# One row of wo per partition loaded early by GpSimd, dealt unevenly over the DMA engines

## The chip, the cores and the metric

The kernel runs on one core of a Trainium2 chip. The metric is the device time of one execution in microseconds (us); the median of three runs stands for the kernel. The profile is one execution taken by the hardware profiler. Data comes from HBM through the 16 DMA engines of the core. A load that is issued by SyncE (SP), ScalarE (ACT) or GpSimd (POOL) is cut into pieces, and each engine works off its own pieces in order. PE is TensorE, DVE is VectorE.

## The reference

One decode step of a block: a layernorm of x (576 numbers), attention of 32 heads over a cache of 16384 keys and values, and a gated MLP beside it, all added up.

```
xn = _layernorm(x, axis=-1)
q = (xn @ wq).reshape(B, Sq, H, Dh)              # H, Dh = 32, 128
scores = einsum("bhqd,bhkd->bhqk", q, k_cache) * Dh**-0.5
o = einsum("bhqk,bhkd->bhqd", softmax(scores), v_cache)
return x + o.reshape(B, Sq, H * Dh) @ wo + (gelu(xn @ w_gate) * (xn @ w_up)) @ w_down
```

The caches are 256 MB each, all of it float32, and everything is read once: 587.6 MB.

## The kernel before, in words

SBUF holds three big slots, A, B and C, each 64 KB per partition. SP issues nearly all loads, in the order of the program, each one when the slot that it fills has been given back: first the weights wq, w_gate and w_up, then for each head 8 MB of keys into A or B and 8 MB of values into C. DVE multiplies and sums keys with the query, PE sums the values. While the last heads are worked off, SP fetches w_down into B and A, and wo behind it.

wo has 4096 rows of 576 numbers. Partition p holds the 32 rows 32p to 32p+31 (`wov`), so that wo is a table of 128 partitions by WO_T = 32 columns j, a column being one row of wo on each partition. The output is the sum over j of a product of one vector of 128 (`oT[:, j]`, the attention's output turned to lie over partitions) with column j. The columns arrive in pieces: 12 and 8 into slot A (`WO_A`), then, once PE has read the last values out of C, 5, 3, 2, 1 and 1 into C (`WO_C`, lines 267 to 271). Each piece has a semaphore of its own, and PE takes the pieces in that order in the loop at line 451.

A load whose destination is 128 partitions gives each DMA engine eight pieces, here eight rows; the load of one column is 128 rows of 2304 bytes, eight on each engine. A load counts as landed when all its engines are done.

The end of the program is a chain over engines. After column j = 25, the first of the piece with three columns, PE signals `s_hf`; DVE adds what two PSUM banks hold into `x2` (lines 369 and 370); PE adds `x2` to the last four accumulators (line 459) and goes through columns 28 to 31; DVE and ACT copy the result out, and ACT stores it. Columns from 26 on (`WO_Q` = 6) go to four accumulators of 144 numbers, the earlier ones to two of 288.

GpSimd only sets constants at the start and then has nothing to do.

Of the kernel before, what the change touches and what calls it, by code (L numbers as in the profile page):

```python
# [8 lines left out]
AF = mybir.ActivationFunctionType  # L9
# [3 lines left out]
P = 128  # L13
H, SK, DH = 32, 16384, 128
D, DF = 576, 4608
# [5 lines left out]
HALF = D // 2  # L21
# [7 lines left out]
WO_T = HD // P  # L29
# [3 lines left out]
LOW, HIGH = 16512, 225280  # L33
WD_B = 28
WO_A = (12, 8)
WO_C = (5, 3, 2, 1, 1)
WO_Q = 6


# [1 line left out]
def kernel(ctx: ExitStack, tc: tile.TileContext, x, k_cache, v_cache, wq, wo, wg, wu, wd, out):  # L41
    nc = tc.nc
    PE, DVE, ACT, SP, PL = nc.tensor, nc.vector, nc.scalar, nc.sync, nc.gpsimd
# [3 lines left out]
    def small(name, shape, where="low"):  # L47
        n = 4
        for s in shape[1:]:
            n *= s  # L50
        h = nc.alloc_sbuf_tensor_at(name, list(shape), F32, offset=at[where])
        at[where] += (n + 31) // 32 * 32
        assert at["low"] <= SLOTS[0] and at["high"] <= 229344
        return h.ap()

    def slot(name, i):
        return nc.alloc_sbuf_tensor_at(name, [P, SLOT], F32, offset=SLOTS[i]).ap()

    A, B, C = slot("slot_a", 0), slot("slot_b", 1), slot("slot_c", 2)
    bank = [nc.alloc_psum_tensor(f"bank{i}", [P, 512], F32).ap() for i in range(8)]  # L60
# [6 lines left out]
    same = small("same", [P, 32])  # L67
# [29 lines left out]
    on = small("on", [P, H])  # L97
    onx = small("onx", [P, P])
    oT = small("oT", [P, WO_T])
    o2 = small("o2", [P, HALF])  # L100
    oTz = small("oTz", [P, WO_Q, 32])
    one31 = small("one31", [1, 32])

    kv = k_cache.rearrange("b h (p n) d -> (b h) p (n d)", p=P)
# [5 lines left out]
    wov = wo.rearrange("(p t) f -> p (t f)", t=WO_T)  # L110
# [4 lines left out]
    def sem(name):  # L115
        return nc.alloc_semaphore(f"{name}_{next(count)}")

    def on_(inst, s, n=1):
        inst.wait_op(s, n, "sem-ge")
        return inst  # L120

    def take(eng, s, n=1):
        eng.wait_ge(s, n).then_inc(s, -n)  # L123
# [6 lines left out]
    def step(eng, inst, after=True):  # L130

        s = own.setdefault(id(eng), None)
        if s is None:
            s = own[id(eng)] = sem("own")
            ahead[id(eng)] = 0
        if after is True:
            after = (s, ahead[id(eng)]) if ahead[id(eng)] else None
        if after:
            on_(inst, *after)
        inst.then_inc(s, 1)  # L140
        ahead[id(eng)] += 1
        return s, ahead[id(eng)]
# [5 lines left out]
    def load(dst, src, s, eng=None):  # L148
        return (eng or SP).dma_start(dst, src).then_inc(s, 16)  # L149
# [21 lines left out]
    s_al, s_pl, s_po, s_mz, s_hf, s_end, s_out = (sem(n) for n in ("al", "pl", "po", "mz", "hf", "end", "out"))  # L171
# [4 lines left out]
    at_c = 0  # L176
    for n in WO_C:
        pieces.append((C, at_c, wov, lo, n))
        at_c, lo = at_c + n, lo + n
    s_tail = [sem("tail") for _ in pieces]  # L180
    acc = [B[:, k * D : (k + 1) * D] for k in range(2)]
    s_wd, s_k0, s_fin = sem("wd"), sem("k0"), sem("fin")

    pgb = bank[:3]
    qgb = bank[3:5]
# [60 lines left out]
    for half_k in range(2):  # L246
        k0 = slice(half_k * SLOT // 2, (half_k + 1) * SLOT // 2)
# [18 lines left out]
    take(SP, fA)  # L266
    for (t, to, src, lo, n), sm in zip(pieces[:-len(WO_C)], s_tail):
        load(t[:, to * D : (to + n) * D], src[:, lo * D : (lo + n) * D], sm)
    take(SP, fV)
    for (t, to, src, lo, n), sm in list(zip(pieces, s_tail))[-len(WO_C):]:  # L270
        load(t[:, to * D : (to + n) * D], src[:, lo * D : (lo + n) * D], sm)
# [5 lines left out]
                                         channel_multiplier=1))  # L277
    cleared = step(PL, PL.memset(whose[:, H:], 0.0), None)
    marked = step(PL, PL.memset(one31[:, 31:], 1.0))


    DVE.wait_ge(s_x, 16)
# [78 lines left out]
    for s in s_acc:  # L361
# [4 lines left out]
    step(DVE, DVE.tensor_mul(on, oall, rl))  # L366
    spread_o = step(DVE, DVE.tensor_mul(onx.rearrange("p (h r) -> p h r", r=4), on.unsqueeze(2).to_broadcast([P, H, 4]),
                                        quarter.unsqueeze(1).to_broadcast([P, H, 4])))
    step(DVE, DVE.tensor_add(x2[:64], x2[:64], half_b[1][64:, :HALF]), (s_hf, 1))  # L369
    x_added = step(DVE, DVE.tensor_add(x2[:64], x2[:64], half_b[0][:64, :HALF]))  # L370
    on_(DVE.tensor_copy(o2[:64, :QUART], acc4[:64]), s_end, 1).then_inc(s_fin, 1)  # L371
# [15 lines left out]
        done(ACT, ACT.activation(oall[:, bass.ds(h, 1)], pcb[:, :1], AF.Copy), own_a)  # L387
    give(ACT, s_al)
    step(ACT, ACT.activation(oT, bank[5][:, :WO_T], AF.Copy), (s_po, 1))
    turned = step(ACT, ACT.activation(oTz[:, :, 31], bank[5][:, WO_T - WO_Q : WO_T], AF.Copy), None)  # L390


    PE.wait_ge(*identity)
# [2 lines left out]
    for j in range(DJ):  # L396
        PE.matmul(bank[5][:, j : j + 1], xm[:, j, :], ones[:1, :1], start=True, stop=True)
    PE.matmul(bank[5][:, DJ : DJ + 1], xd.rearrange("o d s -> o (d s)"), ones[:1, :1], start=True,
              stop=True).then_inc(s_px, 1)
# [9 lines left out]
    with PE.Fori(0, H):  # L409
# [7 lines left out]
        for k in range(32):  # L417
            q = 32 * (k % 4)
            i = PE.matmul(PO[q : q + 4, :], pe[:, 4 * k : 4 * k + 4], C[:, k * 512 : (k + 1) * 512],  # L419
                          start=k < 4, stop=k >= 28)  # L420
# [11 lines left out]
    half = [[half_b[i][32 * (2 * i + j) : 32 * (2 * i + j) + 1, :HALF] for j in range(2)] for i in range(2)]  # L432
    quart = [acc4[32 * g : 32 * g + (1 if g % 2 else 32), :] for g in range(4)]

    def add_out(groups, lhs, w, last=False, after=None):
        n = D // len(groups)
        for k, gr in enumerate(groups):
            lo = k % 2 * HALF + k // 2 * n
            i = PE.matmul(gr, lhs[k % len(lhs)], w[:, lo : lo + n], start=id(gr) not in seen, stop=last)  # L439
            seen.add(id(gr))  # L440
            if after and k == 0:
                on_(i, *after)
        return i

    for k, j in enumerate(range(WD_B, WD_T)):
        add_out(half[j % 2], [hT[:, j : j + 1]], A[:, k * D : (k + 1) * D], after=None if k else (s_tail[0], 16))
    on_(PE.matmul(bank[5][:, :WO_T], onx, same, start=True, stop=True), *spread_o).then_inc(s_po, 1)
    for k in range(2):
        add_out(half[k], [ones[:, :1]], acc[k])
    PE.wait_ge(*turned)  # L450
    for (t, to, _, lo, n), sm in list(zip(pieces, s_tail))[1:]:
        for k, j in enumerate(range(lo, lo + n)):
            w = t[:, (to + k) * D : (to + k + 1) * D]
            if j == WO_T - 4:
                PE.wait_ge(*x_added)
                PE.wait_ge(*marked)
                for i, gr in enumerate(quart):
                    r, c = 32 * (i % 2), i // 2 * QUART
                    PE.matmul(gr, ones[r : r + 1, :1] if i % 2 else one31, x2[r : r + 1, c : c + QUART], start=False,  # L459
                              stop=False)  # L460
            whole = j < WO_T - WO_Q
            lhs = [oT[:, j : j + 1]] if whole else [oTz[:, j - WO_T + WO_Q, :], oT[:, j : j + 1]]
            i = add_out(half[j % 2] if whole else quart, lhs, w,
                        last=j >= WO_T - WO_Q - 2 if whole else j == WO_T - 1, after=None if k else (sm, 16))
            if j == WO_T - WO_Q - 1:
                i.then_inc(s_hf, 1)
    i.then_inc(s_end, 1)

# [33 lines left out]
```

## Time and profile before

| | |
|---|---|
| median of 3 runs | 1362.09 us (1362.01 to 1362.15) |
| the profiled execution | 1362.08 us, of which the span of the profile is 1360.6 us |
| moved | 587.60 MB on SP's queue, 432 GB/s over the span |
| DVE busy | 85% of the span |
| PE busy | 31% of the span |

The profile's queue numbers: q1 is SP's queue, q10 is ACT's, q8 and q14 are fetches of instructions. The busy share of the DMA engines is a mean over 16: a share of 0.25 is four of them at work.

### The profile page before, as it was taken

What the parts mean: (1) busy time and instruction counts of PE and PEld (TensorE: products, weight loads), DVE (VectorE), ACT (ScalarE), POOL (GpSimd) and SP (SyncE); (2) the same over time, 40 slices, a digit from 0 to 9 for tenths busy, and PEclk for the clock granted to TensorE, in tenths of its full rate; (3) what the DMA queues carried; (4) which work ended last, traced back from release to release, by engine and by line L of the source; (5) the groups of instructions that cost most, each with busy time, mean ns of one, the idle gap of its engine ahead of it and who ended that gap; (6) DMA issues with size and microseconds to landing.
All of it is one profiled execution on the core that took longest, in us unless ns stands there. A gap on an engine that the chain in (4) does not pass through costs nothing. (4 is left out here: it accounts for less than half of the span.)

```text
span 1360.6 us, 7958 instructions
## 1 busy us (share of the span) xinstructions
PE 428.4 (31%) x3000; PEld 139.6 (10%) x3000; DVE 1159.9 (85%) x200; ACT 71.9 (5%) x233; POOL 1.5 (0%) x13
## 2 busy tenths in 40 slices
PE   3530233333222333333213333332223333222237
PEld 1110111101000111100001111000001111000012
DVE  1169999999888988898888888998898889988992
ACT  0000000000000000000000000000000000000000
POOL 0000000000000000000000000000000000000000
PEclk9765666666556666665566666665566666655668
DMA  9999999999999999999999999999999999999998
GB/s 399 450 424 432 432 434 447 435 434 434 432 432 434 434 434 432 432 435 447 435 432 434 432 432 435 434 432 432 432 441 441 435 434 432 432 432 435 433 428 379
DMA packets 11824, 587.70 MB, mean 432 GB/s; under 512 B 1317, under 2 KB 1321, under 8 KB 1834
## 3 DMA queue, kind: packets, MB, share of 16 engines
q1 hardware_dynamic: 11808, 587.60, 99.8%
q8 instruction: 5, 0.08, 0.0%
q10 hardware_dynamic: 10, 0.01, 0.0%
q14 instruction: 1, 0.01, 0.0%
HBM read 587.60 MB, written 0.00 MB: 432 GB/s over the span
## 5 line engine op out<-in xcount | busy, mean ns | idle before, releaser
L419 PE MATMUL bank<-slot_c,pe 128*4 128x512 f32 x2048 | 292.4, 735 | 624.1 <-PEq L123 624.1
L220 DVE TENSOR_TENSOR slot_a<-slot_a,qs 128x16384 f32<-128x16384 f32 x16 | 275.6, 17226 | 33.5 <-DVEq L123 33.5
L220 DVE TENSOR_TENSOR slot_b<-slot_b,qs 128x16384 f32<-128x16384 f32 (+1 forms) x17 | 275.8, 16222 | 27.3 <-DVEq L123 27.2
L225 DVE TENSOR_REDUCE s<-slot_b 128x128 f32<-128x16384 f32 (+1 forms) x17 | 275.7, 16216 | 5.7 <-DVEq L123 5.7
L225 DVE TENSOR_REDUCE s<-slot_a 128x128 f32<-128x16384 f32 x16 | 275.5, 17220 | 5.6 <-DVEq L123 5.6
L419 PEld LDWEIGHTS bank<-slot_c,pe 128*4 128x4 f32 x2048 | 56.6, 98 | 832.8 <-issue 832.8
L385 ACT ACTIVATE o<-bank 128x512 f32<-128x512 f32 x32 | 19.1, 597 | 890.5 <-ACTq L123 890.5
L412 PE MATMUL bank<-ident,pm 128*1 128x128 f32 x32 | 11.9, 372 | 168.5 <-PEq L123 168.5
L424 PE MATMUL bank<-same,o 128*128 128x1 f32 x256 | 32.7, 249 | 28.9 <-PEq L123 28.9
L424 PEld LDWEIGHTS bank<-same,o 128*128 128x128 f32 x256 | 31.0, 191 | 57.7 <-issue 57.7
L210 PE MATMUL bank<-qh,ones 128*128 128x128 f32 x66 | 20.1, 396 | 51.4 <-PEq L123 51.4
L319 DVE TENSOR_TENSOR slot_c<-bank,same 128x396 f32<-128x396 f32 (+1 forms) x6 | 3.3, 558 | 37.7 <-PE bank L201 37.5
L229 DVE TENSOR_REDUCE nm<-bank 1x1 f32<-1x128 f32 x32 | 8.9, 279 | 21.5 <-DVEq L123 21.5
L414 PE MATMUL bank<-nm,ones 1*128 1x1 f32 x64 | 17.7, 343 | 18.5 <-PEq L123 18.5
L412 PEld LDWEIGHTS bank<-ident,pm 128*1 128x1 f32 x32 | 2.5, 79 | 175.2 <-issue 175.2
L359 DVE SCALAR_TENSOR_TENSOR slot_b<-slot_b,hT 128x576 f32<-128x576 f32 x26 | 19.0, 810 | 0.0
L414 PEld LDWEIGHTS bank<-nm,ones 1*128 1x128 f32 x64 | 15.9, 307 | 27.9 <-issue 27.9
L210 PEld LDWEIGHTS bank<-qh,ones 128*128 128x128 f32 x66 | 13.1, 248 | 54.6 <-issue 54.6
L305 DVE TENSOR_TENSOR slot_c<-bank,same 128x512 f32<-128x512 f32 x2 | 1.4, 692 | 20.1 <-PE bank L201 20.1
L227 DVE TENSOR_REDUCE pm<-s 128x1 f32<-128x128 f32 x32 | 9.2, 286 | 7.6 <-DVEq L123 7.6
L206 ACT ACTIVATE qh<-qd,whose 128x128 f32<-128x128 f32 x33 | 13.2, 401 | 41.6 <-DVE qd L309 28.2
L380 ACT ACTIVATE nb<-bank 128x1 f32<-128x1 f32 x32 | 5.5, 172 | 179.2 <-ACTq L123 179.2
(88 smaller groups left out, 134.8 us busy)
## 6 DMA issues: line engine op xcount, KB each, us to landing
slot_b<-in_A_k_cache_dram SPq DMA_DIRECT2D x2, 4096.0 KB, 22.4
slot_b<-in_B_w_down_dram SPq DMA_DIRECT2D x1, 8064.0 KB, 41.7
slot_b<-in_B_w_gate_dram SPq DMA_DIRECT2D x1, 6912.0 KB, 54.6
slot_a<-in_B_w_up_dram SPq DMA_DIRECT2D x1, 6912.0 KB, 39.5
slot_a<-in_A_wo_dram SPq DMA_DIRECT2D x1, 3456.0 KB, 35.6
slot_c<-in_B_w_gate_dram SPq DMA_DIRECT2D x1, 2304.0 KB, 28.0
slot_c<-in_B_w_up_dram SPq DMA_DIRECT2D x1, 2304.0 KB, 35.2
slot_a<-in_B_w_down_dram SPq DMA_DIRECT2D x1, 2304.0 KB, 27.8
```

Source lines behind the costliest of these rows:

```text
L206: ACT.activation(qh, qd4.rearrange("p j t -> p (j t)"), AF.Copy, scale=whose[:, bass.ds(h, 1)]).then_inc(s_r, 1)
L210: PE.matmul(pqb[:, :DH], ones, qh, start=True, stop=True).then_inc(qp, 1)
L220: done(DVE, DVE.tensor_mul(blk, blk, qs.unsqueeze(1).to_broadcast([P, n, DH])), own_d)
L225: done(DVE, DVE.tensor_reduce(S[:, i * n : (i + 1) * n], blk, axis=AX.X, op=ALU.add), own_d)
L227: DVE.reduce_max(pm, S, axis=AX.X).then_inc(s_pm, 1)
L229: DVE.tensor_reduce(nm, ptb[:1, :P], axis=AX.X, op=ALU.max, negate=True).then_inc(s_nm, 1)
L359: DVE.scalar_tensor_tensor(acc[k], B[:, bass.ds((2 * i + k + 2) * D, D)], hT[:, bass.ds(2 * i + k + 2, 1)], acc[k], op0=ALU.mult, op1=ALU. ...
L385: ACT.activation(o4, PO, AF.Copy).then_inc(s_o4, 1)
L412: PE.transpose(ptb[:1, :P], pm, ident).then_inc(s_pt, 1)
L414: PE.matmul(ptb[:, 256:257], ones[:1, :], nm, start=True, stop=True).then_inc(s_pb, 1)
L419: i = PE.matmul(PO[q : q + 4, :], pe[:, 4 * k : 4 * k + 4], C[:, k * 512 : (k + 1) * 512], start=k < 4, stop=k >= 28)
L424: i = PE.matmul(pcb[:, :1], o4[:, j * DH : (j + 1) * DH], same[:, j : j + 1], start=j == 0, stop=j == 3)
```

## The change

GpSimd, after its last constant, issues five loads. Three of them bring column 31 of wo, one row of wo per partition of the old layout, into a buffer of its own, `w31`. The rows are dealt out anew: 72 rows as 6 groups of 12, 48 rows as 4 groups of 12, 8 rows as 2 groups of 4. Ahead of the first and of the second of these stands a tiny load (8 rows of 8 bytes, then one number) into `aim`, whose content nothing uses. SP's first piece into slot C is shorter by one column (4 instead of 5), so that SP loads 31 columns. Since the rows of `w31` lie on other partitions than before, DVE copies `onx` into `onp` in the same new order (three copies, L383), PE turns `onp` into `oT[:, 31]` by a product of its own, and the product with `w31` comes ahead of the columns in C. The roles that columns 25 to 31 had are now those of 24 to 30. `o2` and `oTz` move to another place in SBUF to make room.

```diff
-WO_C = (5, 3, 2, 1, 1)
+WO_C = (4, 3, 2, 1, 1)
+WO_L = WO_T - 1
...
+    onp = small("onp", [P, P])
+    w31 = small("w31", [P, D])
+    aim = small("aim", [P, 4])
...
+    shares = ((0, 0, 10, 6, 12), (72, 6, 10, 4, 12), (120, 120, 2, 2, 4))
...
     marked = step(PL, PL.memset(one31[:, 31:], 1.0))
+    for (to, first, gap, k, n), skip in zip(shares, (8, 1, 0)):
+        if skip:
+            at_s, w_s = (0, 2) if skip > 1 else (2, 1)
+            load(aim[:skip, at_s : at_s + w_s], wd[:skip, :w_s], s_aim, PL)
+        src = wov[first // gap * gap : first // gap * gap + gap * n, WO_L * D :]
+        src = src.rearrange("(b a) f -> a b f", a=gap)[first % gap : first % gap + k]
+        load(w31[to : to + k * n, :], src, s_w31, PL)
...
+    for to, first, gap, k, n in shares:
+        base = first // gap * gap
+        dealt = step(DVE, DVE.tensor_copy(
+            onp[:, to : to + k * n].rearrange("p (a b) -> p a b", a=k),
+            onx[:, base : base + gap * n].rearrange("p (b a) -> p a b", a=gap)[:, first % gap : first % gap + k]),
+            spread_o if to == 0 else None)
...
-    on_(PE.matmul(bank[5][:, :WO_T], onx, same, start=True, stop=True), *spread_o).then_inc(s_po, 1)
+    on_(PE.matmul(bank[5][:, :WO_L], onx, same[:, :WO_L], start=True, stop=True), *spread_o)
+    on_(PE.matmul(bank[5][:, WO_L:WO_T], onp, same[:, WO_L:], start=True, stop=True), *dealt).then_inc(s_po, 1)
...
     for (t, to, _, lo, n), sm in list(zip(pieces, s_tail))[1:]:
+        if t is C and not to:
+            PE.wait_ge(s_aim, 32)
+            add_out(half[1], [oT[:, WO_L:]], w31, after=(s_w31, 48))
```

On GpSimd, at the start of the program (`aim` and `w31` as above, `w_99` being `w31`), these rows stand in the change; before, the first two were its last:

```order
L283 MEMSET whose 128x1
L284 MEMSET one_101 1x1
L153 DMA aim<-in_B_w_down_dram 8x2
L153 DMA w_99<-in_A_wo_dram 72x1x576
L153 DMA aim<-in_B_w_down_dram 1x1
L153 DMA w_99<-in_A_wo_dram 48x1x576
L153 DMA w_99<-in_A_wo_dram 8x1x576
```

Nothing stands behind the five loads on this engine. On PE, in the tail behind the last head, before:

```order
L447 MATMUL bank<-same,onx 128x32
L439 MATMUL bank<-slot_b,ones 1x288 x4
L439 MATMUL bank<-slot_a,oT 1x288 x40
L439 MATMUL bank<-slot_c,oT 1x288 x12
L439 MATMUL bank<-slot_c,oTz 32x144
```

and in the change:

```order
L465 MATMUL bank<-same,onx 128x31
L466 MATMUL bank<-same,onp 128x1
L457 MATMUL bank<-slot_b,ones 1x288 x4
L457 MATMUL bank<-slot_a,oT 1x288 x40
L457 MATMUL bank<-w_99,oT 1x288 x2
L457 MATMUL bank<-slot_c,oT 1x288 x10
L457 MATMUL bank<-slot_c,oTz 32x144
```

One product is new (L466), and two products moved from slot C's first piece to `w31`, ahead of it.

## Rows read from the trace of the kernel before

**Rows 1.** The page: span, DMA busy tenths in 40 slices, fetches of instructions.

```profile
span 1360.6 us, 7958 instructions
...
DMA  9999999999999999999999999999999999999998
...
q8 instruction: 5, 0.08, 0.0%
```

**Rows 2.** The chain that ended last: start us, us, what.

```profile
1342.62 13.12 DMA slot_c<-in_A_wo_dram
...
1355.78 0.68 PE bank L439 x5
...
1356.48 0.47 DVE x L369
...
1356.97 0.46 DVE x L370
...
1357.47 0.44 PE bank L459 x6
1357.91 1.16 PE bank L439 x28
...
1359.10 0.30 DVE o L371
```

**Rows 3.** Windows at the end: busy by engine, clock, DMA share, GB/s.

```profile
1356.40:1356.60 0.20, 0.20 (x10) 0.19 (x4) 0.12 (x1) 0.00 (x0) 0.00 (x0) 1.00 0.93 369
...
1357.00:1357.20 0.20, 0.00 (x0) 0.00 (x0) 0.20 (x1) 0.00 (x0) 0.00 (x0) 1.00 0.32 127
1357.20:1357.40 0.20, 0.00 (x0) 0.00 (x0) 0.20 (x1) 0.00 (x0) 0.00 (x0) 1.00 0.30 115
1357.40:1357.60 0.20, 0.13 (x4) 0.13 (x8) 0.02 (x1) 0.00 (x0) 0.00 (x0) 1.00 0.26 104
...
1358.00:1358.20 0.20, 0.20 (x12) 0.20 (x8) 0.00 (x0) 0.00 (x0) 0.00 (x0) 1.00 0.09 35
```

**Rows 4.** DMA packets of 1357.4 to 1357.9.

```profile
DMA packets 23, 0.05 MB, mean 101 GB/s; under 512 B 1, under 2 KB 1, under 8 KB 23
```

**Rows 5.** DMA queues of 44 to 50: packets, MB, share of 16 engines.

```profile
q8 instruction: 1, 0.02, 1.0%
```

**Rows 6.** DMA queues of 1350 to 1358.4, same columns.

```profile
q8 instruction: 1, 0.02, 0.7%
```

**Rows 7.** DMA queues of 1358.4 to 1361, same columns.

```profile
q8 instruction: 1, 0.02, 2.2%
q10 hardware_dynamic: 4, 0.00, 0.3%
```

**Rows 8.** Timeline of GpSimd, its last instruction: start us, us, what.

```profile
3.68 0.09 POOL L279 MEMSET one<- 1x1 f32 x1
```

**Rows 9.** Timeline of the tail on DVE and PE, idle time in brackets.

```profile
1341.81 1.02 PE L424 MATMUL bank<-same,o 128*128 128x1 f32 x8 [0.90 <-PEq L123]
...
1344.78 0.29 DVE L367 TENSOR_TENSOR onx<-on,quarter 128x128 f32<-128x128 f32 x1
...
1347.44 0.41 PE L447 MATMUL bank<-same,onx 128*128 128x32 f32 x2
...
1348.30 5.03 PE L439 MATMUL bank<-slot_a,oT 128*1 128x288 f32 x80
...
1353.65 1.62 PE L439 MATMUL bank<-slot_c,oT 128*1 128x288 f32 x20 [0.32 <-DMA slot_c<-in_A_wo_dram]
```

**Rows 10.** Timeline of PE at its last column.

```profile
1358.58 0.30 PE L439 MATMUL bank<-slot_c,oT 128*1 128x144 f32 x2
```

More of the change, by code (lines that the diff above doesn't have):

```diff
@@ L99 @@
     oT = small("oT", [P, WO_T])
-    o2 = small("o2", [P, HALF])
-    oTz = small("oTz", [P, WO_Q, 32])
+    o2 = small("o2", [P, HALF], "high")
+    oTz = small("oTz", [P, WO_Q, 32], "high")
+    onp = small("onp", [P, P])
+    w31 = small("w31", [P, D])
+    aim = small("aim", [P, 4])
     one31 = small("one31", [1, 32])
@@ L181 @@
     acc = [B[:, k * D : (k + 1) * D] for k in range(2)]
-    s_wd, s_k0, s_fin = sem("wd"), sem("k0"), sem("fin")
+    s_wd, s_k0, s_fin, s_w31, s_aim = sem("wd"), sem("k0"), sem("fin"), sem("w31"), sem("aim")
+    shares = ((0, 0, 10, 6, 12), (72, 6, 10, 4, 12), (120, 120, 2, 2, 4))
     pgb = bank[:3]
@@ L389 @@
     step(ACT, ACT.activation(oT, bank[5][:, :WO_T], AF.Copy), (s_po, 1))
-    turned = step(ACT, ACT.activation(oTz[:, :, 31], bank[5][:, WO_T - WO_Q : WO_T], AF.Copy), None)
+    turned = step(ACT, ACT.activation(oTz[:, :, 31], bank[5][:, WO_L - WO_Q : WO_L], AF.Copy), None)
     PE.wait_ge(*identity)
@@ L451 @@
     for (t, to, _, lo, n), sm in list(zip(pieces, s_tail))[1:]:
+        if t is C and not to:
+            PE.wait_ge(s_aim, 32)
+            add_out(half[1], [oT[:, WO_L:]], w31, after=(s_w31, 48))
         for k, j in enumerate(range(lo, lo + n)):
             w = t[:, (to + k) * D : (to + k + 1) * D]
-            if j == WO_T - 4:
+            if j == WO_L - 4:
                 PE.wait_ge(*x_added)
@@ L460 @@
                               stop=False)
-            whole = j < WO_T - WO_Q
-            lhs = [oT[:, j : j + 1]] if whole else [oTz[:, j - WO_T + WO_Q, :], oT[:, j : j + 1]]
+            whole = j < WO_L - WO_Q
+            lhs = [oT[:, j : j + 1]] if whole else [oTz[:, j - WO_L + WO_Q, :], oT[:, j : j + 1]]
             i = add_out(half[j % 2] if whole else quart, lhs, w,
-                        last=j >= WO_T - WO_Q - 2 if whole else j == WO_T - 1, after=None if k else (sm, 16))
-            if j == WO_T - WO_Q - 1:
+                        last=j >= WO_L - WO_Q - 2 if whole else j == WO_L - 1, after=None if k else (sm, 16))
+            if j == WO_L - WO_Q - 1:
                 i.then_inc(s_hf, 1)
```

## The prediction

> **What bounds the kernel now.** I read the page first. In all but the last of the 40 slices the DMA engines are at nine tenths or more [rows 1]: the kernel moves its bytes without a pause, and the reader is to see that no compute engine can be the bound before the tail. So only the tail, and how evenly the 16 engines reach it, can change the time. The chain that ended last comes next. It leaves the DMA at 1342.62 + 13.12 = 1355.74, when the piece with wo's columns 25 to 27 has landed, and from there runs through PE (0.68), two additions on DVE (0.47 and 0.46), PE with x (0.44) and PE with the last four columns (1.16) to the copies at 1359.10 [rows 2]. Nothing in it waits for another load, but the last load is close behind: PE starts on its last column at 1358.58 [rows 10], and DMA is at work until some time between 1358.0 and 1358.2 [rows 3].
>
> The windows at the end say who is late there. The DMA share is 0.93 until 1356.6, then 0.32, 0.30 and 0.26, and the last packets go before 1358.2 [rows 3]. A share of 0.26 is four engines of 16. So some eleven engines have finished their part of the last load before 1357.0, a fifth late one (0.30 × 16 = 4.8 engines) at about 1357.35, and four finish only at 1358.0 to 1358.2, about a microsecond after most. Each load counts as landed with its slowest engine, so those four set every landing of the tail, also that of 1355.74.
>
> Why four? The page counts five fetches of instructions [rows 1], and one of these runs after 1358.4 [rows 7], so four came before the end of the loads. A fetch costs its engine about a microsecond: 1.0% of 16 engines in 6 us is 0.96 us [rows 5], and 0.7% in 8.4 us is 0.94 us [rows 6]. Four fetches of 0.95 us and four engines a microsecond late fit each other. No view names the engine of a packet, so that fetches and late engines are the same is inferred.
>
> **The change part by part.** *SP's tail is one column shorter.* The price of a row is read where only the late engines work: from 1357.4 to 1357.9 there are 23 packets, one of them tiny [rows 4], so four engines do 22 rows in 0.5 us, 4 × 0.5 / 22 = 0.091 us a row. Every engine has eight rows less in the tail: −0.73 us in every landing from slot C's first piece on.
>
> *GpSimd's three loads give rows back, at the start.* An engine that carries 12 rows is 12 × 0.091 = 1.09 us behind for the rest of the program, since no slack follows [rows 1]; one with 4 rows 0.36 us, one with none 0. Against SP's eight, ten engines (6 + 4) are 0.36 us worse, two are 0.36 us better, and four are 0.73 us better. GpSimd is idle from 3.77 us on [rows 8], and the rows are needed only after 1353, so the issue itself waits for nobody and nothing queues behind it.
>
> *Five more completions, two tiny loads.* The trace has no load from GpSimd. The nearest row is the store: four packets on q10 in 0.3% of 16 engines in 2.6 us, 0.125 us [rows 7]. Two are rows of half the length (0.045 us each by the price above), which leaves 0.017 us for each of the other two. Five completions on each engine would be 0.09 us; the bounds are 0 and, with the whole packet's mean of 0.031 us, 0.16. The tiny rows are of the same size and go into that bound.
>
> *DVE's three copies* begin after `onx`, which ends at 1344.78 + 0.29 = 1345.07, and PE asks for it at 1347.44 [rows 9]. Three copies of at most 128x128, 0.29 us each by that same row, end by 1345.94. Free, with 1.5 us of cover.
>
> *PE* gets one more product (two instructions; eight such took 1.02 us, so 0.26 us) and takes `w31` (four instructions at 5.03 / 80 = 0.063, 0.25 us) ahead of slot C [rows 9]. Before, PE had stood idle for 0.32 us until 1353.65 for C's first piece. Now it is through slot A's rows at 1353.33 + 0.26 = 1353.59, through `w31` at 1353.84, and through the four columns of C's first piece (16 × 0.063) at 1354.85, if that piece has landed, which it has (1353.65 − 0.64 = 1353.01). The next piece lands at 1355.74 − 0.64 = 1355.10. So the additions on PE are hidden, but with only 0.25 us left. Were that cover gone, PE would be the bound and the gain would shrink by what PE is over.
>
> *Sum.* If the four late engines are those that get no rows: −0.73 + 0.09 = −0.64 us on the landing at 1355.74, and all of the chain behind it moves by as much. The last load moves with it, and PE's last column too, so their order holds. The fifth engine decides the rest: it is about 0.8 us ahead of the latest, and with 12 rows it moves by +0.36 + 0.09 = +0.45, so it would become last and the gain would be 0.8 − 0.45, about 0.35 to 0.4; with 4 rows it drops out. I take −0.6, near the full size, because the 0.8 is a rough reading of shares while 0.64 is counted. On the profiled execution, 1362.08 (span 1360.6, 1.5 around it, which nothing here touches), this gives 1361.48; the median of 1362.09 is the same within 0.01.
>
> [...] The rows say that the end is four engines' affair, so that it matters which engine gets a row [rows 3, 4]. [...]
>
> **The rivals.**
>
> *The rows hit late engines.* Nothing in the trace shows on which engine GpSimd starts, nor which are late. If one late engine gets 12 rows, it is +0.36 + 0.09 = 0.45 us worse, and since the chain follows the slowest, the kernel takes 1362.5. For it: the four that are spared have to be exactly the four that fetch instructions; one miss is enough. A further fetch of 0.95 us that comes before the end, because the program got longer, has nearly the same price on an engine with 12 rows (1357.0 + 0.45 + 0.95 = 1358.4 against 1358.2). Against it: eight rows of tiny size and then one look like steps that put the loads in chosen places. That is the change's intention and no evidence, so the chance stays at 0.22.
>
> *The loads are spread over all 16 engines.* Then the change does not do what it says: 128 rows over 16 are eight on each, or nine where rounding adds one, and the late engines get back what they lost: −0.73 + 0.73 to 0.82 + 0.09 = +0.1 to +0.2, that is 1362.2. The store of two rows left as two data packets and two completions [rows 7], which speaks for few engines where rows are few, but that is ACT's queue. Chance 0.13. [...]
>
> *Few engines carry all of it* (the other side). If the 72 rows went to one engine, it would have 72 × 0.091 = 6.55 us of them; on an engine that is a microsecond early this is 6.55 − 0.73 − 1.0 = 4.8 us late, 1366.9. It decides from some 18 rows on one engine (1.0 + 0.73 − 0.09 = 1.64 us), and passes 0.2% from about 48. The division into 6, 4 and 2 groups speaks against it. Chance 0.04.
>
> *PE becomes the bound.* It has 0.25 us left above; were each matmul a tenth slower, the 6.5 us from 1348.30 on would grow by 0.65, be 0.4 over, and leave a gain of 0.24, 1361.8. PE's granted clock in the tail is 1.00 [rows 3], which speaks against it. Chance 0.06.
>
> **How the numbers follow.** Forecast 0.55, late engines hit 0.22, spread evenly 0.13, PE 0.06, one engine overloaded 0.04. The likeliest gives 1361.5 (its own range 1361.3 to 1361.8). The range of 1361.3 to 1362.6 takes in the hit on late engines and the even spread. About 0.2%, 2.7 us, is what a measurement of this kernel can tell from no change; only the last case passes it on the slow side, and nothing found here could on the fast side: equal ends for all engines would win about 0.8 us at most (four engines' microsecond shared by 16 leaves a quarter of it). Faster 0.01, same 0.95, slower 0.04.
>
> **What the profile after would show.** Right: the share at the end falls from 0.9 to near 0 within about half a microsecond, instead of a step at 0.26 that lasts 1.2; the chain's DMA step ends near 1355.1 and still leads into PE, DVE, PE. A step of 0.06 or more (one engine or several) that lasts as long as before, or longer, says that late engines were hit. An unchanged step at 0.25 says that the rows were spread evenly. A chain that shows PE without a wait between slot A and the copies says that PE bounds. A fetch count on q8 other than five before and after 1358 would make the inference about late engines wrong.

## The result, and the profile after

The change takes 1364.51 us (median of 20 runs, 1363.59 to 1366.46 but for one), the kernel before in the same runs 1362.12 (1361.95 to 1362.52): a ratio of 1.0019 (95% interval 1.0012 to 1.0026), 2.4 us slower. Forecast were 1361.5 and a range up to 1362.6. One of the 20 runs took 2443.1 us and is left out of the comparison. The profiled execution took 1364.65.

The page of the change, with the lines that answer to [rows 1]; behind a queue stand packets, MB and share of 16 engines:

```profile
span 1363.2 us, 7971 instructions
...
DMA  9999999999999999999999999999999999999998
...
q1 hardware_dynamic: 11808, 587.31, 99.7%
q0 software_dynamic: 336, 0.30, 0.1%
q8 instruction: 5, 0.08, 0.0%
```

The span is 2.6 us longer, with the same bytes and the same nines in the DMA row. A new queue, q0, is GpSimd's. Five fetches, as before. The chain that ended last (start, duration, what), against [rows 2]:

```profile
1345.00 13.28 DMA slot_c<-in_A_wo_dram
...
1358.33 0.68 PE bank L457 x5
...
1359.03 0.47 DVE x L387
...
1359.52 0.46 DVE x L388
...
1360.02 0.44 PE bank L481 x6
1360.46 1.19 PE bank L457 x26
...
1361.67 0.30 DVE o L389
```

The same chain with nearly the same durations, 2.6 us later in every step from PE on. Its DMA step already begins 2.4 us later (1345.00 against 1342.62), before anything of the shorter tail has been moved. So most of the time was lost ahead of the tail. Where, the loads of the start say: KB, and us from issue to landing, of the kernel before

```profile
slot_b<-in_B_w_gate_dram SPq DMA_DIRECT2D x1, 6912.0 KB, 54.6
...
slot_b<-in_A_wq_dram SPq DMA_DIRECT2D x1, 1024.0 KB, 22.9
```

and of the change:

```profile
slot_b<-in_B_w_gate_dram SPq DMA_DIRECT2D x1, 6912.0 KB, 56.8
...
slot_b<-in_A_wq_dram SPq DMA_DIRECT2D x1, 1024.0 KB, 25.8
w<-in_A_wo_dram POOLq DMA_DIRECT2D x1, 162.0 KB, 20.7
w<-in_A_wo_dram POOLq DMA_DIRECT2D x1, 108.0 KB, 23.8
```

The second is 2.9 us late, the first, which lands last of the loads that SP issues in the first 6 us, still 2.2: most of the loss is made in the first 30 us and stays. What the engines do in this time is seen when busy share and bytes are read side by side. Windows of the kernel before (the last two columns are the DMA share and GB/s; a packet, the unit in which an engine moves data, counts in the window in which it starts, so a short window's share can pass 1):

```profile
24.00:28.00 4.00, 2.65 (x16) 0.80 (x20) 0.00 (x0) 0.00 (x0) 0.00 (x0) 1.00 1.03 440
...
8.00:40.00 32.00, 13.13 (x90) 5.40 (x90) 7.36 (x20) 0.39 (x2) 0.00 (x0) 0.99 0.94 405
```

and of the change:

```profile
24.00:28.00 4.00, 0.00 (x0) 0.00 (x0) 0.00 (x0) 0.00 (x0) 0.00 (x0) 1.00 1.12 358
28.00:32.00 4.00, 3.71 (x20) 1.12 (x24) 0.00 (x0) 0.00 (x0) 0.00 (x0) 1.00 0.95 378
32.00:36.00 4.00, 4.00 (x32) 1.06 (x28) 0.00 (x0) 0.00 (x0) 0.00 (x0) 1.00 1.04 442
...
8.00:40.00 32.00, 14.10 (x90) 5.54 (x90) 3.81 (x15) 0.29 (x1) 0.00 (x0) 1.00 0.96 383
```

The engines are as busy as before and move less: 358 GB/s at a share of 1.12, where they moved 440 at 1.03. The work is not waiting; its packets take longer, until about 32 us: those of 64 KB 2.61 to 2.81 us where they start from 16 to 20 us (before: 2.42), those of 18 KB 0.83 to 1.06 us from 24 to 28 (before: 0.69), and from 32 us on all are as before. A reader who looks at the nines of the page alone sees no difference.

### The profile page after: what moved, and what is told of

The parts are those of the page before. It is cut to its first block, busy times and chain, and to the rows that moved or that the text cites. A ratio compares the mean times of both kernels' runs of the same rounds, so it can differ in the third digit from the quotient of the medians.

```text
span 1363.2 us, 7971 instructions
## 1 busy us (share of the span) xinstructions
PE 427.2 (31%) x3002; PEld 139.1 (10%) x3002; DVE 1160.3 (85%) x203; ACT 71.9 (5%) x233; POOL 4.5 (0%) x18
## 5 line engine op out<-in xcount | busy, mean ns | idle before, releaser
L206 PE MATMUL bank<-slot_a,xnb 128*32 128x512 f32 (+2 forms) x136 | 14.3, 575 | 1.5 <-DMA slot_a<-in_B_w_up_dram 1.5
```

The lines of the kernel that those rows point to most:

```text
L206: i = PE.matmul(banks[b][32 * q : 32 * q + 32, :size], lhs, rhs[:, lo : lo + size], start=k == 0, stop=k == len(steps) - 1)
```

## The experiments

All were timed in five rounds beside the kernel before, which took 1362.13 to 1362.24 in them. A time is a median; behind it stand the lowest and the highest of 11 runs, and the ratio with its 95% interval. That interval is about 0.1% to either side, 1.2 us: smaller differences are read from how the runs lie and from the trace, not from the ratio. Where a load is added that nothing uses, PE waits for it before its last columns; in e5 and in e9 to e12 `o2` and `oTz` lie where the change has them.

**Which part of the loads?** Two loads by themselves, added to the kernel before (label e1):

```diff
     marked = step(PL, PL.memset(one31[:, 31:], 1.0))
+    load(aim[:8, :2], wd[:8, :2], s_aim, PL)
+    load(aim[:1, 2:3], wd[:1, :1], s_aim, PL)
```

> The kernel before, plus GpSimd's two tiny loads at the start (8 rows of 8 bytes, then one number), which nothing uses; wo comes by SP alone. Theory S1 (each load that GpSimd issues slows all 16 engines' packets for a while, whatever it moves; five loads cost 1.8 us): two of five, +0.7 us, and SP's packets between 10 and 30 us take longer than before. Theory S2 (the slowing goes with the rows that GpSimd's queue moves): +0.0 to +0.1 us, no slow packets. Theory A (only the late engines were hit by rows): 0.0 us.

Measured: 1362.2 (1362.05 to 1362.38), 1.0001 (0.9992 to 1.001). That GpSimd issues these two loads costs nothing that can be told.

**Who issues, and in what order?** In the change, column 31 by one plain load of 128 rows in the old order, without the copies on DVE and the product on PE, issued by GpSimd (e2) or by ACT (e3):

```diff
-    for (to, first, gap, k, n), skip in zip(shares, (8, 1, 0)):
...
+    load(w31, wov[:, WO_L * D :], s_w31, PL)      # e3: ACT
```

> As the change, but column 31 comes by one plain load of 128 rows from GpSimd, in the old order: no tiny loads, no new deal of rows, no copies on DVE. Theory S1: one load of five, 0.37 us of slowing, eight rows of 0.1 us given back for the 0.73 us won in the tail: +0.4 to +0.5 us against the kernel before. Theory S2: 1.8 us of slowing and 0.1 us more for the rows: +1.9 to +2.1 us. Theory A: rows are even, +0.1 us. Theory P (rows that lie ten rows apart are slow to read, whoever asks): the order is plain, 0.0 to +0.1 us, no slow packets.

> As the run with one plain load of 128 rows, but issued by ACT behind its loads of x, on the queue q10, not by GpSimd. Theories S1 and S2 (GpSimd's queue is what slows): no packet of SP's is slowed, -0.73 us in the tail and +0.73 at the start: 0.0 us, within 0.1. If the same rows early are slow by any queue: +1.8 us as in the change.

Measured: 1362.25 (1362.04 to 1362.69), 1.0001 (0.9992 to 1.001), and 1362.15 (1361.98 to 1362.27), 1.0000 (0.9991 to 1.0009). The windows of the first of them:

```profile
24.00:28.00 4.00, 1.82 (x12) 0.59 (x16) 0.00 (x0) 0.00 (x0) 0.00 (x0) 1.00 1.04 446
...
8.00:40.00 32.00, 13.12 (x90) 5.35 (x90) 6.68 (x18) 0.29 (x1) 0.00 (x0) 1.00 0.96 410
```

Full rate, with the same 128 rows from the same queue. So neither the queue nor the bytes slow the rest.

**Does it follow the loads?** The change with its five loads issued only after `hidden`, just ahead of DVE's first head, at 87.6 us (e4), and the kernel before with the five loads added and their rows unused (e5):

```diff
     hidden = step(DVE, DVE.scalar_tensor_tensor(hT, t2, 0.5, u, op0=ALU.mult, op1=ALU.mult))
+    PL.wait_ge(*hidden)
+    for (to, first, gap, k, n), skip in zip(shares, (8, 1, 0)):
```

> The change as it is, but GpSimd waits with its five loads until DVE has made the MLP's hidden vector (about 84 us), so that only packets of 64 KB and 32 KB stand beside them. Theories S1 and S2: the slowing is there at about 84 to 100 us instead of 17 to 30; if it is a share of the time (8 to 11% as of 64 KB packets), 1.0 to 1.4 us of it, kernel +1.3 to +2.4 us. If the loss came from something at the start of the program (code, wq's small rows), no packet is slowed and the kernel is at -0.3 to +0.5 us.

> The kernel before with GpSimd's five loads of the change added, whose content nothing uses: SP still loads all 32 columns, no copies on DVE, no other product on PE. Theory D (engines that get no rows of a load on few engines do small placeholder packets instead, and these slow all 16 engines): the change's loss without its 0.73 us in the tail, 2.4 + 0.7 = +3.1 us. If the copies, the product or the shorter tail cost something of their own: less than +2.5 us.

Measured: 1364.71 (1364.08 to 1366.72), 1.0021 (1.0012 to 1.003), and 1364.83 (1364.17 to 1365.47), 1.002 (1.0011 to 1.0029). The late loads' windows:

```profile
24.00:28.00 4.00, 2.58 (x15) 0.73 (x19) 0.00 (x0) 0.00 (x0) 0.00 (x0) 1.00 1.06 455
...
90.00:140.00 50.00, 3.16 (x15) 1.02 (x19) 47.85 (x7) 0.94 (x4) 0.65 (x2) 0.50 1.02 416
```

and that of the kernel before:

```profile
90.00:140.00 50.00, 7.20 (x43) 1.85 (x47) 47.85 (x7) 0.94 (x4) 0.00 (x0) 0.52 1.02 440
```

The start is now at full rate, and the loss stands at 90 to 140 us: 416 GB/s where the kernel before moves 440 at the same share. It goes where the loads go, and at 2.6 us it is a little over the range that was expected. The loads alone, without the shorter tail, cost 2.7 us, which lies between the two expectations (+3.1, and less than +2.5). Read against the change's 2.4 it leaves the shorter tail 0.3 us instead of 0.73; both kernels' runs spread over more than that difference, and no run here settles it.

**Idle engines' packets, evenness, the queue again.** Three more: 64 rows of 8 bytes dealt as two groups by GpSimd (e6), added to the kernel before; the change's column dealt as 16 groups of 8, 16 rows apart, in one load by GpSimd, so that every engine has the same (e7); the change's three loads issued by ACT, without the tiny ones (e8).

```diff
+    load(aim[:64, :2], wd[:64, :2].rearrange("(b a) f -> a b f", a=2), s_aim, PL)    # e6
...
-    shares = ((0, 0, 10, 6, 12), (72, 6, 10, 4, 12), (120, 120, 2, 2, 4))
+    shares = ((0, 0, 16, 16, 8),)                                                    # e7
...
-        load(w31[to : to + k * n, :], src, s_w31, PL)
+        load(w31[to : to + k * n, :], src, s_w31, ACT)                               # e8
```

> The kernel before, plus one load by GpSimd of 64 rows of 8 bytes in 2 groups of 32, which nothing uses: half a kilobyte in all. Theory D: 14 engines without rows do 16 placeholder packets each, 224 beside the change's 160, and all 16 engines' packets take 5 to 30% longer for some 10 us or more: +1.8 to +3.5 us. [...]

> As the change, but the 128 rows are dealt as 16 groups of 8, rows 16 apart in wo, each engine writing 8 neighbouring partitions, by one load from GpSimd and without the tiny loads: all 16 engines have rows. Theory D: no placeholders, no slow packets, 0.0 to +0.2 us. [...]

> The change's three loads of rows (6 x 12, 4 x 12, 2 x 4), in the same order, issued by ACT instead of GpSimd and without the tiny loads. [...]

Measured: e6 1362.36 (1362.18 to 1362.57), 1.0001 (0.9992 to 1.001); e7 1363.52 (1363.14 to 1365.56), 1.0012 (1.0003 to 1.0021); e8 1364.86 (1364.59 to 1365.59), 1.002 (1.0011 to 1.0029). The windows of e8:

```profile
28.00:32.00 4.00, 4.00 (x24) 1.13 (x20) 0.00 (x0) 0.00 (x0) 0.00 (x0) 1.00 0.99 362
32.00:36.00 4.00, 4.00 (x36) 1.13 (x32) 0.00 (x0) 0.00 (x0) 0.00 (x0) 1.00 1.01 356
36.00:40.00 4.00, 3.10 (x32) 0.73 (x24) 0.69 (x1) 0.00 (x0) 0.00 (x0) 1.00 1.05 441
```

From ACT's queue the same loads do the same harm, and longer. Even dealing does it too, if less: +1.4 us, which lies above theory D's range. Theory D falls: ACT's queue has 17 packets under 512 bytes in e8, where GpSimd's has 272 in the change, and the harm is as large; and e7 loses with rows on all engines (80 packets on GpSimd's queue, 64 of two rows and 16 small ones). The counts fit a dealing of one group to an engine: in e8 ACT's queue has 140 packets more than in the kernel before, the 128 rows and 6 + 4 + 2 small ones; in the change 168 packets of GpSimd's queue have 8 bytes, the 8 of the tiny load and 160, which is 10 × 6 + 12 × 6 + 14 × 2, one for each pair of rows that an engine goes without. The tiny rows of e6 cost 0.2 us, but they test less than was meant, since their queue shows 32 packets and not the 224 placeholders of the expectation. What is left is the dealing itself: either that one engine reads rows that lie far apart (theory R), or that an engine writes partitions that an ordinary load leaves to another (theory W).

**Reading or writing?** The kernel before with two unused loads by ACT: the same 64 rows, the same 8 groups, and only the destination differs.

```diff
+    for to, first in ((0, 0), (32, 32)):        # e10: ((64, 0), (96, 32))
+        src = wov[first : first + 32, (WO_T - 1) * D :].rearrange("(b a) f -> a b f", a=8)
+        load(w31[to : to + 32, :], src, s_w31, ACT)
```

> The kernel before, and in addition two unused loads by ACT, each of 32 rows of wo's column 31, read 8 rows apart in 8 groups of 4; 64 rows in all, 8 on each of 8 engines. They are written to partitions 0 to 31 and 32 to 63. Theory W (writing): the slowing comes from engines that write partitions which an ordinary load of 128 partitions leaves to other engines; here the 8 lowest engines write partitions that they also write in ordinary loads, so no packet of SP is slowed, and the kernel costs only the rows, 8 x 0.091 = 0.73 us where one of the late engines is among these, nothing where none is: 1362.1 to 1362.9, and 64 KB packets stay at 2.42 us. Theory R (reading): it comes from one engine reading rows that lie far apart; then half the rows of the even experiment at least halve its +1.4 us, and come on top: 1362.9 to 1363.5, with packets of SP above 2.6 us while the rows come.

> [...] Theory W: slow packets (64 KB above 2.6 us) while the rows come, and +0.7 to +1.4 us over the kernel before, 0.5 us or more above the twin that writes its own partitions. Theory R: the same time as that twin within 0.2 us, and the same packets.

Measured: to partitions 0 to 63, 1362.59 (1362.17 to 1363.2), 1.0004 (0.9995 to 1.0013); to partitions 64 to 127, 1363.76 (1362.87 to 1364.35), 1.0011 (1.0002 to 1.002). The first one's landing and window:

```profile
slot_b<-in_B_w_gate_dram SPq DMA_DIRECT2D x1, 6912.0 KB, 54.5
```

```profile
8.00:40.00 32.00, 13.12 (x90) 5.37 (x90) 6.78 (x18) 0.29 (x1) 0.00 (x0) 1.00 0.95 408
```

and the second one's:

```profile
slot_b<-in_B_w_gate_dram SPq DMA_DIRECT2D x1, 6912.0 KB, 55.5
```

```profile
8.00:40.00 32.00, 13.81 (x90) 5.61 (x90) 4.80 (x17) 0.29 (x1) 0.00 (x0) 1.00 0.94 392
```

The first run lies in theory W's range and below theory R's; the second, at +1.6 us, is 0.2 above W's. In both, ACT's queue has 90 packets, 80 more than in the kernel before: 64 rows, and eight small ones for each load. That fits eight engines to a load; which eight, and which partitions they write in an ordinary load, is theory W's supposition, and no view shows it. The runs of the two overlap a little (1363.2 and 1362.87), but their packets do not. The windows of 12 to 16 us, first one and second one:

```profile
12.00:16.00 4.00, 2.42 (x10) 2.36 (x10) 2.46 (x10) 0.00 (x0) 0.00 (x0) 1.00 1.23 533
```

```profile
12.00:16.00 4.00, 2.42 (x10) 2.36 (x10) 2.40 (x11) 0.01 (x1) 0.00 (x0) 1.00 1.33 533
```

The same bytes take 8% more engine time. The trace keeps start, size and duration of every packet: of the 32 packets of 64 KB that start in this window, all take 2.42 us in the first run, and all take 2.54 to 2.69 in the second, so the slowing is not one of a few engines. The same reading costs 1.17 us more when it is written elsewhere. R falls.

**Is it the place, or whose place?** Four unused loads by GpSimd of 32 rows, all 128 rows, 8 groups each. Both kernels write the same rows to the same partitions; only the order of the loads differs. If GpSimd takes the engines in turn, which is supposed here and not shown, the order decides which 8 engines write which partitions.

```diff
+    for to, first in ((0, 0), (64, 64), (32, 32), (96, 96)):    # e12: (64, 64), (0, 0), (96, 96), (32, 32)
+        src = wov[first : first + 32, (WO_T - 1) * D :].rearrange("(b a) f -> a b f", a=8)
+        load(w31[to : to + 32, :], src, s_w31, PL)
```

> The kernel before, and in addition four unused loads by GpSimd of 32 rows each (all 128 rows of column 31, 8 groups of 4, read 8 rows apart), written to partitions 0 to 31, 64 to 95, 32 to 63 and 96 to 127 in this order. Each load takes 8 engines. If GpSimd starts at the lowest engine and goes on with the next 8, every engine writes its own partitions. Theory W: then no slow packets and only 8 rows on every engine, 0.73 us, 1362.9; were the start another, slow packets and 1363.4 to 1364.4. Theory R: slow packets whatever the order, 1363.5 to 1364.4.

> The same four loads by GpSimd with the pairs exchanged: partitions 64 to 95, 0 to 31, 96 to 127, 32 to 63, and the rows with them. Theory W: if GpSimd starts at the lowest engine, every engine now writes partitions of another; slow packets and 1363.4 to 1364.4, 0.5 us or more above the other order. Theory R: the same time as the other order within 0.2 us.

Measured: low partitions first 1362.87 (1362.69 to 1363.09), 1.0005 (0.9996 to 1.0014); high first 1364.64 (1364.26 to 1365.17), 1.0018 (1.0009 to 1.0027). Low first:

```profile
slot_b<-in_B_w_gate_dram SPq DMA_DIRECT2D x1, 6912.0 KB, 55.2
```

```profile
24.00:28.00 4.00, 1.73 (x12) 0.50 (x16) 0.00 (x0) 0.00 (x0) 0.00 (x0) 1.00 1.04 440
...
8.00:40.00 32.00, 13.12 (x90) 5.35 (x90) 6.60 (x18) 0.29 (x1) 0.00 (x0) 1.00 0.95 407
```

High first:

```profile
slot_b<-in_B_w_gate_dram SPq DMA_DIRECT2D x1, 6912.0 KB, 57.3
```

```profile
24.00:28.00 4.00, 0.00 (x0) 0.00 (x0) 0.00 (x0) 0.00 (x0) 0.00 (x0) 1.00 1.06 368
...
8.00:40.00 32.00, 13.80 (x90) 5.60 (x90) 3.90 (x16) 0.29 (x1) 0.00 (x0) 1.00 0.96 386
```

Low first costs what eight rows cost: 8 × 0.091 = 0.73 us by the prediction's price, and the medians differ by 0.73. High first costs 1.77 us more, 0.2 above the end of theory W's range, for the same bytes in the same places; none of its 11 runs comes near one of the other order. So the place by itself is not the cause. Both runs have 192 packets on GpSimd's queue, 64 of two rows and 32 small ones for each load: 16 as for any load, and 16 that fit two for each of eight engines without rows. That the order decides which engine writes it is inferred, since no view names the engine of a packet. The reading changes hands with the order too; that it is the writing rests on the pair by ACT.

**The change without that (e13).** All of the change, but column 31 in the four loads of the good order, even, and without the tiny loads; DVE's copies follow the new order.

```diff
-    shares = ((0, 0, 10, 6, 12), (72, 6, 10, 4, 12), (120, 120, 2, 2, 4))
+    shares = ((0, 0), (64, 64), (32, 32), (96, 96))
...
+    for to, first in shares:
+        src = wov[first : first + 32, WO_L * D :].rearrange("(b a) f -> a b f", a=8)
+        load(w31[to : to + 32, :], src, s_w31, PL)
```

> The change mended: GpSimd brings all of column 31 in four loads of 32 rows (8 groups of 4, read 8 rows apart) into partitions 0 to 31, 64 to 95, 32 to 63, 96 to 127, in this order, with the copies on DVE, the product on PE and SP's shorter piece as in the change, and without the two tiny loads. Theory W: every engine writes its own partitions, so no packet is slowed; each engine has 8 rows more at the start and 8 fewer in the tail, -0.73 + 0.73, and four completions of up to 0.1 us: 1362.1 to 1362.3, more than 2 us below the change, the chain's last DMA step ending at 1355.7 to 1355.9. Rival V: something else in the change (the copies, the product, the moved buffers, the dealt order on PE) has part in its +2.4; then this kernel keeps that part: 1362.8 or more, or a chain that runs through other work than that of before.

Measured: 1362.25 (1362.13 to 1364.08), the kernel before beside it 1362.24; 1.0002 (0.9993 to 1.0011). Its chain, and its windows:

```profile
1341.96 13.73 DMA slot_c<-in_A_wo_dram
...
1355.73 0.68 PE bank L451 x5
```

```profile
8.00:40.00 32.00, 13.46 (x90) 5.49 (x90) 6.37 (x18) 0.29 (x1) 0.00 (x0) 1.00 0.94 404
```

```profile
1357.20:1357.60 0.40, 0.18 (x8) 0.14 (x8) 0.17 (x1) 0.00 (x0) 0.00 (x0) 1.00 0.31 121
1357.60:1358.00 0.40, 0.40 (x16) 0.21 (x12) 0.00 (x0) 0.00 (x0) 0.00 (x0) 1.00 0.23 92
```

The loss is gone, and with even shares nothing is gained: the DMA step ends at 1355.69 (before: 1355.74), and the step of four late engines stands at the end as it did in [rows 3]. Rival V, that something else of the change has part in the loss, falls too.

## Why the prediction was wrong

**The step that failed** is "GpSimd's three loads give rows back, at the start": "An engine that carries 12 rows is 12 × 0.091 = 1.09 us behind [...]; one with 4 rows 0.36 us, one with none 0." It charged each row to the engine that carries it and to no other. The runs show a second price, which is not paid by the carrying engines alone: while the dealt rows are under way, the transfers beside them are slower. Its size from the windows of 8 to 40 us, as GB/s for each unit of busy share (an estimate): 404 / 0.94 = 430 in the mended change, 383 / 0.96 = 399 in the change, 7.2% less; of 0.96 × 32 = 30.7 busy microseconds that is 2.2 us, give or take 0.3 since the share has two digits. The pair with the two orders gives 407 / 0.95 = 428 and 386 / 0.96 = 402, 6.1% or 1.9 us, and 1.77 by its times. No row of the kernel before could have priced this, since all its big loads are ordinary ones; but the sum then had to carry a bound for transfers beside the rows, and it had none.

The packet records give the second price more sharply. SP's packets that start from 5 to 45 us, each against the median of its size in the kernel before, added up and divided by 16 engines, take longer by 1.9 us in the change, 1.9 in the high order, 0.9 in e7 and 1.0 in ACT's run to partitions 64 to 127; by 0.1 or less in the low order, in ACT's run to 0 to 63, in e2 and in the mended change.

Why the order of loads decides no view shows, since none names the engine of a packet. The runs fit theory W if ACT's groups go to the same eight engines in both of its runs, and GpSimd's loads to these and to the other eight in turn, as the author supposed: ACT's groups cost +0.45 us on 0 to 63 and +1.6 on 64 to 127 (1362.59 and 1363.76 against 1362.14), and GpSimd's loads cost +0.73 with the low partitions first and +2.5 with the high ones first. In the change, 72 rows go to partitions 0 to 71 in blocks of 12, and in e7 all go in blocks of eight neighbours; that engines write partitions of others there too is inferred from the slowing alone.

Why such a write should slow everybody isn't shown either. 368 GB/s at a share of 1.06 (high first, 24 to 28 us) says that the engines are busy and move less, and no run here tells one cause of that from another.

**The rest of the 2.4 us.** By the windows 2.2 of it, give or take 0.3, is the common slowing, by the packets 1.9 of the 2.6 us that the profiled execution is longer. What is left, 0.2 to 0.7, has room for the rival "the rows hit late engines" (0.45 us) and none for the gain of 0.6. Where the dealing is even the same account closes: 1.9 and 0.73 are 2.6, and the high order's span is 2.6 longer (1363.2 against 1360.6). So the rest goes with uneven shares, as far as single executions tell. For the rival speaks also the end of the change; the DMA row and GB/s in 40 slices of 1357.0 to 1361.2 us:

```profile
DMA  9989989998989977665232332322221000000070
GB/s 373 483 329 373 373 351 571 373 373 329 395 329 373 373 285 285 263 263 198 88 132 110 132 154 110 132 88 110 88 88 44 22 22 22 22 22 0 0 156 0
```

A slice is 0.105 us. From the 20th, at 1359.0, to 1360.1 the share is still 0.2 to 0.3, three to five engines, and one or two go on until 1360.8. The prediction had named this sign: a step at the end that lasts as long as before means that late engines were not spared. Which engines are late, and whether the tiny loads put the shares where they were meant to be, no run shows; how large that part is stays open. An uneven dealing in which every engine writes only its own partitions was not tried. In the last load of the kernel before, each of the four late engines does eight packets of 2304 bytes, 0.0895 us apart, and then one of 4 bytes; that is eight partitions of the 128, and 12 rows in eight partitions need a second buffer. For its 2304 bytes per partition this kernel has no room left (736 and 96 bytes in its two areas for small tensors).

**The other steps.** *The price of a row* was right: 0.73 us forecast for eight rows, 0.73 between the medians (low partitions first), though the ratio's interval alone would allow −0.5 to +1.9 us. GpSimd's packets bring two rows each and take 0.178 us in the mended change, 0.089 a row; in the change they take 0.211. *SP's tail one column shorter* was right in the mended change (e13): what that adds early it gets back there, 1362.25 against 1362.24. In the change itself it is worth 0.3 by the medians of e5 and the change, and why is open. *The loads and completions themselves* are small: two tiny loads cost less than 0.1 us, and a packet of 4 bytes on GpSimd's queue takes 0.010 us in the change. *DVE's copies and PE's product are hidden*, as forecast. The timeline of the change on DVE and on PE:

```profile
1347.25 0.41 DVE L383 COPY onp<-onx 128x72 f32<-128x72 f32 x3
```

```profile
1348.25 0.41 PE L465 MATMUL bank<-same,onx 128*128 128x31 f32 x2
1348.49 0.36 PE L466 MATMUL bank<-same,onp 128*128 128x1 f32 x2
...
1355.45 0.66 PE L457 MATMUL bank<-w,oT 128*1 128x288 f32 x4
1356.26 1.15 PE L457 MATMUL bank<-slot_c,oT 128*1 128x288 f32 x15
```

The three copies take 0.41 us together and are done 0.6 us before PE starts the two products. PE is through C's first columns at 1357.4, 0.9 us before the piece that the chain waits for: PE did not become the bound. *No gain*, the time of the kernel before, is what came where the rows were even and plain or in the fitting order (1362.15 to 1362.25 in e2, e3 and e13), and not with the change. *The rivals*: neither the time of the even spread (1362.2) nor that of one engine with all rows (1366.9) was met; no run shows the nine rows on an engine behind the 0.82 of the even spread, and e2's plain load has 64 packets of two rows and 16 small ones on GpSimd's queue, which fits eight rows on each; the rival on the slow side was too narrow, since it looked for a single overloaded engine, and not for a price on all.

## What to carry to other kernels

A transfer that is dealt out by hand can have two prices, its own rows and what it does to the transfers beside it; the second shows where busy share and GB/s are read together, because the slowed engines here looked as busy as fast ones (383 GB/s at a share of 0.96, before 405 at 0.94). In a kernel that has no DMA slack, a small load that is cut otherwise than its neighbours can cost several times its own time: here 128 rows, 0.73 us on each engine, cost 2.5 in the wrong order. Where rows are dealt to chosen engines, try the same loads in the other order as a test, which was worth 1.77 us here. That it is best when each engine writes the partitions that it writes anyway is what these runs suggest, and an inference.

## What the runs showed that was not expected

- The rate of all engines together falls from 440 to 358 GB/s at a full busy share while 0.3 MB of dealt rows are under way, and is back when these have landed.
- From ACT's queue the same three loads depress the rate until 36 us (356 GB/s from 32 to 36); from GpSimd's it is over by 32 (442).
- 64 rows of 8 bytes, dealt as two groups, cost 0.2 us by the medians (1362.36 against 1362.16).
- The change's runs spread over 2.9 us (1363.59 to 1366.46), those of the kernel before over 0.6; the mended change and the low order stay near the latter but for one run of 1364.08. Why was not looked into.
